# A seventh pair of heads ahead of the first feed-forward, and weight sizes on VectorE alone

## The chip, the core and the metric

One core of one Trainium2 chip runs the kernel. The metric is the device time of one execution in microseconds (us). Three timed runs of the kernel before are given, and one profiled execution of it.

## What is computed

`reference()` chains two parts. The first is attention in which a query sees only the keys of its own hash bucket; the second is a gated feed-forward with a convolution of three taps along the sequence.

```python
q_bits = (np.einsum('bhsd,dk->bhsk', q, proj) > 0)       # the same for k
mask = q_bucket[:, :, :, None] == k_bucket[:, :, None, :]
scores = np.where(mask, scale * np.matmul(q, k.transpose(0, 1, 3, 2)), -1000000000.0)
scores = scores - np.max(scores, axis=-1, keepdims=True)
attn = np.exp(scores); attn = attn / (np.sum(attn, axis=-1, keepdims=True) + 1e-09)
x = np.matmul(attn, v)                                    # heads side by side: [4, 768, 512]
h = np.maximum(x @ w_in, 0.0)                             # [512, 1024]
out = (h * sigmoid(conv3(h)) @ w_out)                     # [1024, 512]
```

There are 4 batches, 8 heads, 768 positions and 64 values per head. q, k and v are float32. The weights w_in, w_out and the taps come as 64-bit floats, which the kernel itself splits into two float32 parts.

## The kernel before

Heads go in pairs: 16 pairs, four per batch. A pair is 12 units, a unit being 128 queries of one head against 768 keys. For each unit TensorE makes the products (L286, into `s`), VectorE takes the row maximum while it copies them to `e` (L299), ScalarE takes the exponential with its sum (L306), and three units later TensorE transposes `e` (L329, into `t`), which ScalarE copies to `at` (L336). `s` and `t` share three PSUM buffers, so the next transposes wait until a maximum has emptied its buffer. Every fourth unit the matmuls with v follow for 256 queries (L355, into `v`): this unit is called a burst here.

The products use a bucket mask in extra rows. For that each pair's R (queries and keys, transposed) is loaded into one single buffer (L191); TensorE makes its hash (L219), VectorE and GpSimd turn it into `bits` (L222, L224), GpSimd splits R into a rounded high part `hi` (L204) and a low part that stays in R (L209), for one head and then for the other. DMAs of the SP queue, in program order, bring these to their rows (L207 `hi`, L211 R, L228 `bits`). `prepare` spreads these steps over units 1 to 7 of the pair in front; the other head's low part (the second L209) falls into the burst at unit 7, after which the next load of R is issued. The hash of a pair stands at unit 3 of the pair in front, in a burst.

The early pairs (six, up to the first feed-forward) leave the softmax's division to the end: VectorE makes reciprocals of the sums (L320, L321), GpSimd spreads them to 64 columns each (`rec`, L323), TensorE transposes them beside the values (L350, two per burst), ScalarE copies them out (L360), VectorE multiplies (`x`, L364), and GpSimd splits x into `xh` and `xl` (L365, L366). The later ten pairs are normalised on GpSimd before the transposes instead (L314).

The weights are 16 blocks of 128 x 512. For each one ScalarE takes the absolute value (L87), GpSimd clamps it (L90), VectorE makes the upper word (L95, L97) and the lower (L102, L104), ScalarE rounds the upper to the high part (L136), and GpSimd makes the low part (L139, L140). The upper word has two buffers. `background` issues these steps, 3.75 VectorE operations in each burst from unit 7 on, and what is left in the first feed-forward. Behind a burst's maximum VectorE's order is: x's product, then this lump of weight operations, then the next maximum.

The feed-forward of a batch follows two pairs (`DEFER`) behind the batch's last: after pairs 5, 9, 13 and 15, counted from 0. It has 16 steps of hidden matmuls (L393), convolution and gate, and output matmuls (L423). The first burst behind each feed-forward's start is the one of the last 256 queries. All engines run in the order in which the program is written.

## Time and profile before

| What | Value |
|---|---|
| three timed runs | 748.12, 752.3, 996.83 us; median 752.3 |
| the profiled execution | 750.76 us, its span 749.0 us |
| busy in the span | TensorE 714.4, VectorE 499.2, ScalarE 509.2, GpSimd 373.6 us |

An engine's busy time is the sum of its own instructions. A busy TensorE is not TensorE at its best, since matmuls are pipelined and a slow clock counts as busy. The order of time of an engine gives the start and the length of instructions of one kind in a row; in brackets stands how long the engine was idle before and who ended the wait. A row's name out<-in is that of the tiles.

### The profile page before, as it was taken

How to read it: one execution, taken by the hardware profiler on the slowest of the kernel's cores; microseconds unless marked ns; L12 is line 12 of the kernel's file. 1: busy time of each engine (PE TensorE's matmuls, PEld its weight loads, DVE VectorE, ACT ScalarE, POOL GpSimd, SP SyncE). 2: the span in 40 equal slices, each digit the busy share in tenths (PEclk: the TensorE clock that was granted, in tenths of full speed). 3: DMA queues.
4: the chain of work that ended last, by engine and by line, in shares of the span. 5: the costliest groups of instructions: out<-in, count | busy, mean ns of one | idle time of the engine just before them, and what ended most of it. 6: DMA issues, size and time to landing. Idle time of an engine off the chain costs nothing.

```text
span 749.0 us, 13385 instructions
## 1 busy us (share of the span) xinstructions
PE 714.4 (95%) x4588; PEld 587.5 (78%) x4588; DVE 499.2 (67%) x1195; ACT 509.2 (68%) x954; POOL 373.6 (50%) x372
## 2 busy tenths in 40 slices
PE   5989999988899999999999999999999999999997
PEld 3767777776679987777788988777788897778986
DVE  7588999977667656666657655665666665564663
ACT  5867887886655548778774557787785547785554
POOL 4366777756566324755735423656645323341221
PEclk8999999998999999999999999999999999999999
DMA  3876576553412102365441302255461211000011
GB/s 141 198 204 155 141 206 181 168 162 85 114 43 72 64 37 70 82 181 136 121 121 31 104 1 105 68 150 132 119 163 33 70 43 63 2 1 1 0 43 43
DMA packets 30357, 72.18 MB, mean 96 GB/s; under 512 B 5937, under 2 KB 7505, under 8 KB 30289
## 3 DMA queue, kind: packets, MB, share of 16 engines
q1 hardware_dynamic: 27696, 62.88, 30.9%
q10 hardware_dynamic: 2592, 8.44, 3.6%
q8 instruction: 37, 0.61, 0.3%
q14 instruction: 32, 0.25, 0.1%
HBM read 27.40 MB, written 6.29 MB: 45 GB/s over the span
## 4 chain that ended last, share of the span: by engine, by line
PE 69%; DVE 4%; POOL 4%; DMA 3%; ACT 1%; issue 1%; SPq 0%; POOLq 0%; DVEq 0%
PE o L423 18%; PE h L393 17%; PE s L286 11%; PE t L329 11%; PE v L355 11%; DVE e L299 2%; DMA k<-R 1%; DMA R<-in_qk 1%; PE hash L219 1%; POOL wuo L139 1%; POOL e L314 1%; POOL wo L140 1%; ACT e L306 1%; DVE wuo L97 1%; POOL R L209 1%
## 5 line engine op out<-in xcount | busy, mean ns | idle before, releaser
L299 DVE TENSOR_SCALAR_CACHE_REDUCE e<-s 128x768 f32<-128x768 f32 x192 | 183.3, 955 | 80.9 <-PE s L286 72.1
L306 ACT ACTIVATE e<-e,st 128x768 f32<-128x768 f32 x192 | 181.2, 944 | 23.1 <-DVE st L303 12.8
L336 ACT COPY at<-t 128x768 f32<-128x768 f32 x192 | 152.3, 794 | 47.3 <-PE t L329 47.1
L329 PE MATMUL t<-ident,e 128*128 128x128 f32 x1152 | 164.5, 280 | 19.9 <-DVE e L299 17.9
L314 POOL TENSOR_SCALAR e<-e,st 128x768 f32<-128x768 f32 x120 | 109.3, 911 | 117.3 <-ACT at L336 59.9
L329 PEld LDWEIGHTS t<-ident,e 128*128 128x128 f32 x1152 | 133.4, 144 | 42.6 <-DVE e L299 22.4
L402 DVE SCALAR_TENSOR_TENSOR ht<-ht,cw 128x384 f32<-128x384 f32 (+1 forms) x128 | 117.8, 921 | 70.0 <-ACT ht L400 66.8
L412 POOL TENSOR_TENSOR g<-ht,g 128x384 fp32r<-128x384 f32 x64 | 72.0, 1125 | 163.9 <-ACT g L411 129.7
L423 PE MATMUL o<-wo,g 128*128 128x512 f32 x576 | 143.3, 395 | 0.7 <-POOL g L412 0.7
L393 PE MATMUL h<-xh,wi 128*128 128x386 f32 x512 | 142.0, 340 | 0.0
L355 PE MATMUL v<-at,v 128*64 128x256 f32 x1152 | 134.9, 383 | 0.0
L423 PEld LDWEIGHTS o<-wo,g 128*128 128x128 f32 x576 | 107.0, 188 | 23.5 <-ACT ht L400 1.2
L286 PE MATMUL s<-K,Q 128*128 128x384 f32 x384 | 118.7, 391 | 1.0 <-POOL K L253 0.9
L355 PEld LDWEIGHTS v<-at,v 128*64 128x64 f32 x1152 | 78.7, 137 | 45.5 <-issue 10.9
L286 PE MATMUL s<-k,q 96*128 96x384 f32 x384 | 102.2, 348 | 2.2 <-DVE e L299 2.2
L405 ACT ACTIVATE ht<-ht 128x384 f32<-128x384 f32 x64 | 33.6, 525 | 96.4 <-DVE ht L402 96.4
L393 PEld LDWEIGHTS h<-xh,wi 128*128 128x128 f32 x512 | 94.0, 188 | 3.7 <-ACT ht L400 1.2
L393 PE MATMUL h<-xl,wi 128*128 128x386 f32 x256 | 86.8, 339 | 0.0
L286 PEld LDWEIGHTS s<-K,Q 128*128 128x128 f32 x384 | 60.1, 196 | 22.2 <-issue 17.4
L286 PEld LDWEIGHTS s<-k,q 96*128 96x128 f32 x384 | 72.9, 197 | 3.0 <-ACT q L266 3.0
L406 DVE TENSOR_TENSOR ht<-ht 128x384 f32<-128x384 f32 x64 | 41.5, 649 | 31.5 <-ACT ht L405 31.3
L209 POOL TENSOR_TENSOR R<-R,hi 128x768 fp32r<-128x768 f32 x30 | 60.4, 2014 | 0.9 <-PE hash L219 0.8
(75 smaller groups left out, 622.2 us busy)
## 6 DMA issues: line engine op xcount, KB each, us to landing
R<-in_qk SPq DMA_DIRECT2D x15, 768.0 KB
K<-hi SPq DMA_DIRECT2D x60, 192.0 KB
v<-in_v SPq DMA_DIRECT2D x16, 384.0 KB
out<-osb SPq DMA_DIRECT2D x24, 256.0 KB
Q<-hi SPq DMA_DIRECT2D x30, 192.0 KB
q<-hi SPq DMA_DIRECT2D x30, 192.0 KB
Q<-R SPq DMA_DIRECT2D x30, 192.0 KB
k<-R SPq DMA_DIRECT2D x30, 192.0 KB
```

Source lines behind the costliest of these rows:

```text
L209: nc.gpsimd.tensor_tensor(lo, R, hi.bitcast(F32), ALU.subtract)
L286: nc.tensor.matmul(self.sp[:, half, :HS], A[:, h, qs], C[:, h, half * HS:(half + 1) * HS], start=(kk == 0), stop=(kk == 1))
L299: nc.vector.tensor_scalar(self.e.rearrange("p (a b) -> p a b", a=2), self.sp[:, :, :HS], MASKED, None, ALU.max, ALU.max, accum_out=self.st ...
L306: nc.scalar.activation(self.e, self.e, AF.Exp, bias=self.st[:, 1:2], scale=SCALE, accum_out=self.sum)
L314: nc.gpsimd.tensor_scalar(self.e, self.e, self.st[:, 3:4], 0.0, ALU.mult, ALU.add)
L329: nc.tensor.transpose(self.tp[:, c // 3, c % 3 * P:(c % 3 + 1) * P], self.e[:, c * P:(c + 1) * P], ident)
L336: nc.scalar.copy(pr.at[self.h][:, :, :, self.tq * P:(self.tq + 1) * P], self.tp[:, :, :3 * P].rearrange("p j (c q) -> p j c q", c=3))
L355: nc.tensor.matmul(av[h * D:(h + 1) * D, :QB], vt[:, c, h, :], ats[h][:, c // 3, c % 3, :], start=(c == 0), stop=(c == NCK - 1), tile_posi ...
L393: nc.tensor.matmul(hp[:, :HW], w, x[:, c0:c0 + HW], start=(n == 0), stop=(n == 3 * NCC - 1))
L402: nc.vector.scalar_tensor_tensor(t[:, a:z], ht[:, o + k - 1 + a:o + k - 1 + z], cw[:, f, k:k + 1], t[:, a:z], ALU.mult, ALU.add)
L412: nc.gpsimd.tensor_tensor(g[:, 1, :], t, g[:, 0, :].bitcast(F32), ALU.subtract)
L423: nc.tensor.matmul(op, l, r, start=(f == 0 and n == 0), stop=(f == NFC - 1 and n == 2))
```

## The change

- `DEFER` goes from 2 to 3: the feed-forwards follow pairs 6, 10, 14 and 15, and seven pairs instead of six divide at the end.
- The size of a weight is made on VectorE: a bitwise and with 0x7FFFFFFF, and a maximum with the smallest size. The absolute value on ScalarE and the clamp on GpSimd go. A block has six VectorE operations, issued 5.2 to a burst, one less at a hash. GpSimd's two operations of a block are issued as soon as the block's last VectorE operation is. Upper and lower words, and the output copies, share four buffers (before: two and five).
- The sums have a second column that holds 1e-9, so one reduction adds it; the spreading on GpSimd goes. Four matmuls take a column of reciprocals, read 64 times, as the weight and the identity as the moving operand.
- x's product overwrites `rs` (two buffers); its two GpSimd operations are issued behind the burst's weight steps.
- `prepare` has two lists: the hash stays where all steps stood, ahead of the burst's value matmuls; the high and low parts of R go behind x's parts.
- The feed-forward's steps fetch no weights any more and issue one weight step instead of two.

```diff
--- before.py
+++ after.py
...
 LAG, EB = 3, 5
-DEFER = 2
+DEFER = 3
 FLAG = 3
 LATE = NP + DEFER
...
-RATE = 3.75
+RATE = 5.2
...
+    sums4 = [cp.tile([P, 2 * QB // P, 2], F32, name=f"sums{i}") for i in range(3)]
+    for t in sums4:
+        nc.gpsimd.memset(t, 1e-9)
...
-            self.up, self.low = (ring(wp, bufs, [P, WC], I32, f"w{x}", f"w{x}{name}")[:, :n]
-                                for x, bufs in (("u", 2), ("l", 5)))
+            self.low, self.up = (ring(wp, 4, [P, WC], I32, "w", f"{x}{name}")[:, :n] for x in ("low", "up"))
             self.upf, self.lowf = self.up.bitcast(F32), self.low.bitcast(F32)
 
-        def size(self):
-            nc.scalar.activation(self.lowf, self.hi.bitcast(F32), AF.Abs)
-
-        def clamp(self):
-            nc.gpsimd.tensor_scalar(self.lowf, self.lowf, F32_MAX, F64_MIN, ALU.min, ALU.max)
-
-        def upper(self):
+        def vector(self):
...
             V, up, low = nc.vector, self.up, self.low
+            V.tensor_scalar(low, self.hi, 0x7FFFFFFF, None, ALU.bitwise_and)
+            yield
+            V.tensor_scalar(self.lowf, self.lowf, F64_MIN, None, ALU.max)
+            yield
             V.tensor_scalar(low, low, 3, 0x3FFFFFFF, ALU.logical_shift_left, ALU.bitwise_and)
             yield
             V.scalar_tensor_tensor(up, self.hi, -0x40000000, low, ALU.bitwise_and, ALU.bitwise_or)
             yield
-
-        def lower(self):
-            V, up, low = nc.vector, self.up, self.low
             V.tensor_scalar(low, up, -0x800000, None, ALU.bitwise_and)
             yield
             V.scalar_tensor_tensor(self.lowf, self.lo, 2.0 ** -52, self.lowf, ALU.mult, ALU.mult)
...
     def split_weights():
-        todo, ends = [], None
-        def ahead():
-            if fetched:
-                raw, name = fetched.pop(0)
-                todo.append(Decode(raw, WC, name))
-                todo[-1].size()
-        ahead()
-        ahead()
-        yield
-        for d in todo:
-            d.clamp()
-        yield
-        while todo:
-            d = todo.pop(0)
-            ahead()
-            yield from d.upper()
-            if ends:
-                ends()
-            if len(todo) == 2:
-                todo[-1].clamp()
-            yield from d.lower()
-            blk = weights[d.name] = cp.tile([P, 2, WC], F32R, tag=f"w{d.name}", name=f"w{d.name}")
+        while fetched:
+            raw, name = fetched.pop(0)
+            d = Decode(raw, WC, name)
+            yield from d.vector()
+            blk = weights[name] = cp.tile([P, 2, WC], F32R, tag=f"w{name}", name=f"w{name}")
             nc.scalar.copy(blk[:, 0, :], d.upf)
-            def ends(d=d, blk=blk):
-                nc.gpsimd.tensor_tensor(d.upf, d.upf, blk[:, 0, :].bitcast(F32), ALU.subtract)
-                nc.gpsimd.tensor_tensor(blk[:, 1, :], d.upf, d.lowf, ALU.add)
-        ends()
+            nc.gpsimd.tensor_tensor(d.upf, d.upf, blk[:, 0, :].bitcast(F32), ALU.subtract)
+            nc.gpsimd.tensor_tensor(blk[:, 1, :], d.upf, d.lowf, ALU.add)
+            yield
...
-            for now in ((sa,), (), (hs, sa), (hs,), (sb,), (), (sb,)):
-                for g in now:
-                    next(g, None)
-                yield
+            def steps(plan):
+                for g in plan:
+                    if g:
+                        next(g, None)
+                    yield
+            return steps((None, None, hs, hs)), steps((sa, None, sa, None, sb, None, sb))
...
         def reciprocals(self):
 
             pr = self.pair
-            sums = self.sums
-            nc.vector.tensor_scalar(sums, sums, 1e-9, None, ALU.add)
-            nc.vector.reciprocal(sums, sums)
-            pr.rec = ring(wp, 1, [P, QB // P, 2, D], F32, "rec", f"rec{self.nm}")
-            nc.gpsimd.tensor_scalar(pr.rec, sums.unsqueeze(3).to_broadcast([P, QB // P, 2, D]), 1.0, 0.0,
-                                    ALU.mult, ALU.add)
+            pr.inv = ring(wp, 2, [P, 2 * QB // P], F32, "inv", f"inv{self.nm}")
+            nc.vector.tensor_reduce(pr.inv, self.sums, mybir.AxisListType.X, ALU.add)
+            nc.vector.reciprocal(pr.inv, pr.inv)
...
             for t in range(QB // P):
-                nc.tensor.transpose(av[:, QB + t * P:QB + (t + 1) * P],
-                                    rec[:, t].rearrange("p h d -> p (h d)"), ident)
+                for h in range(2):
+                    nc.tensor.matmul(av[h * D:(h + 1) * D, QB + t * P:QB + (t + 1) * P],
+                                     inv[:, 2 * t + h:2 * t + h + 1].to_broadcast([P, D]), ident,
+                                     start=True, stop=True, tile_position=(0, h * D))
...
         def out():
-            x = ring(wp, 1, [P, QB], F32, "x32", f"x{pr.nm}_{qb}")
-            nc.vector.tensor_tensor(x, av[:, :QB], rs, ALU.mult)
-            nc.gpsimd.tensor_scalar(xh[:, cols], x, 1.0, 0.0, ALU.mult, ALU.add)
-            nc.gpsimd.tensor_tensor(xl[:, cols], x, xh[:, cols].bitcast(F32), ALU.subtract)
+            nc.vector.tensor_tensor(rs, av[:, :QB], rs, ALU.mult)
+        def parts():
+            nc.gpsimd.tensor_scalar(xh[:, cols], rs, 1.0, 0.0, ALU.mult, ALU.add)
+            nc.gpsimd.tensor_tensor(xl[:, cols], rs, xh[:, cols].bitcast(F32), ALU.subtract)
...
-        rs = ring(wp, 1, [P, QB], F32, "rs", f"rs{pr.nm}_{qb}")
-        return [spread, *chunks], (factors, out)
+        rs = ring(wp, 2, [P, QB], F32, "rs", f"rs{pr.nm}_{qb}")
+        return [spread, *chunks], (factors, out, parts)
...
-            fetch(1)
             background(1)
             if i >= 3:
-                next(prep[0], None)
+                prepare(0)
+                prepare(1)
...
             if i < len(todo):
                 gs.append(next(run[i]))
-            background(1)
...
+        parts = []
         if burst:
-            for high, low in lows:
+            for high, low, part in lows:
                 low()
+                parts.append(part)
             lows = []
         if u and k == PREP and pi + 1 < len(pairs):
-            prep[0] = pairs[pi + 1].prepare()
-        next(prep[0], None)
+            prep[:] = pairs[pi + 1].prepare()
+        prepare(0)
+        if ending:
+            prepare(0)
         for _ in range(1 + NCK if ending else AVS[(i - LAG) % 4]):
             if av:
                 steps, last = av[0]
...
                     outs.append(last)
                     av.pop(0)
         if burst and i >= W0:
-            background(RATE)
+            background(RATE - (k == PREP + 2))
+        for last in parts:
+            last()
+        prepare(1)
```

VectorE in the burst at unit 7 of the sixth pair (1_1): `x` and `rs` are the product of the values, `wl`, `wu` or `low`, `up` a block's lower and upper words, `e` the next units. Before:

```order
L364 TENSOR_TENSOR x1_0_2_2208<-v1_0_2_2047,rs1_0_2_2048 128x256
L102 TENSOR_SCALAR wlo5_1857<-wuo5_1856 128x512
L104 SCALAR_TENSOR_TENSOR wlo5_1857<-rawo5_1601,wlo5_1857 128x512
L95 TENSOR_SCALAR wlo6_1977<-wlo6_1977 128x512
L97 SCALAR_TENSOR_TENSOR wuo6_1976<-rawo6_1731,wlo6_1977 128x512
L299 TENSOR_SCALAR e1_1_4_0_2252,st1_1_4_0_2250<-s1_1_4_0_2245 128x768
L303 TENSOR_SCALAR st1_1_4_0_2250<-st1_1_4_0_2250 128x1
```

and now:

```order
L333 TENSOR_TENSOR rs1_0_2_2019<-v1_0_2_2018,rs1_0_2_2019 128x256
L93 TENSOR_SCALAR lowo4_2072<-lowo4_2072 128x512
L95 TENSOR_SCALAR lowo4_2072<-lowo4_2072 128x512
L97 SCALAR_TENSOR_TENSOR upo4_2073<-rawo4_1471,lowo4_2072 128x512
L99 TENSOR_SCALAR lowo4_2072<-upo4_2073 128x512
L101 SCALAR_TENSOR_TENSOR lowo4_2072<-rawo4_1471,lowo4_2072 128x512
L270 TENSOR_SCALAR e1_1_4_0_2221,st1_1_4_0_2220<-s1_1_4_0_2215 128x768
```

Four weight operations of three blocks became five of one block, whose size is made here too. Whatever stands between x's product and the next `e` delays that maximum.

GpSimd in the same burst: `hi` and R are the parts for the next pair, `w...` the weight block, `xh` and `xl` the parts of x. Before:

```order
L204 TENSOR_SCALAR hi1_2_1_2160<-R1_2_1863 128x768
L365 TENSOR_SCALAR xh1_0_1808<-x1_0_2_2208 128x256
L366 TENSOR_TENSOR xl1_0_1809<-x1_0_2_2208,xh1_0_1808 128x256
L209 TENSOR_TENSOR R1_2_1863<-R1_2_1863,hi1_2_1_2160 128x768
L139 TENSOR_TENSOR wuo4_1722<-wuo4_1722,wo4_2102 128x512
L140 TENSOR_TENSOR wo4_2102<-wuo4_1722,wlo4_1723 128x512
L90 TENSOR_SCALAR wlo7_2105<-wlo7_2105 128x512
```

and now:

```order
L171 TENSOR_SCALAR hi1_2_1_2129<-R1_2_1838 128x768
L111 TENSOR_TENSOR upo4_2073<-upo4_2073,wo4_2199 128x512
L112 TENSOR_TENSOR wo4_2199<-upo4_2073,lowo4_2072 128x512
L336 TENSOR_SCALAR xh1_0_1779<-rs1_0_2_2019 128x256
L337 TENSOR_TENSOR xl1_0_1780<-rs1_0_2_2019,xh1_0_1779 128x256
L176 TENSOR_TENSOR R1_2_1838<-R1_2_1838,hi1_2_1_2129 128x768
```

R's low part stood ahead of the two weight operations and stands behind them and behind x's parts now; the clamp of a later block (L90) is gone. L111 reads what ScalarE rounds after the block's last VectorE operation.

## Rows read from the trace of the kernel before

**Rows 1.** The page's part 1: busy us, share of the span, instructions of each engine.
```profile
PE 714.4 (95%) x4588; PEld 587.5 (78%) x4588; DVE 499.2 (67%) x1195; ACT 509.2 (68%) x954; POOL 373.6 (50%) x372
```

**Rows 2.** TensorE in order of time: start us, us, line, operation, tiles, count.
```profile
24.76 2.81 PE L355 MATMUL v<-at,v 128*64 128x256 f32 x24
...
207.44 2.81 PE L355 MATMUL v<-at,v 128*64 128x256 f32 x24
...
634.26 2.81 PE L355 MATMUL v<-at,v 128*64 128x256 f32 x24
...
642.78 2.81 PE L355 MATMUL v<-at,v 128*64 128x256 f32 x24
```

**Rows 3.** Who TensorE waited for: us in total, times, longest us.
```profile
PE t L329 <- DVE e L299: 17.9, 13, 3.5
...
PE hash L219 <- DMA R<-in_qk: 2.1, 4, 1.0
```

**Rows 4.** VectorE in order of time, 185 to 192 us; idle time in brackets.
```profile
185.50 0.94 DVE L95 TENSOR_SCALAR wlo<-wlo 128x512 int32<-128x512 int32 x1
190.73 0.69 DVE L97 SCALAR_TENSOR_TENSOR wuo<-rawo,wlo 128x512 int32<-128x512 int32 x1 [4.29 <-POOL wo L140]
191.34 0.95 DVE L299 TENSOR_SCALAR_CACHE_REDUCE e<-s 128x768 f32<-128x768 f32 x1
```

**Rows 5.** GpSimd in order of time, the same stretch.
```profile
186.12 2.00 POOL L209 TENSOR_TENSOR R<-R,hi 128x768 fp32r<-128x768 f32 x1
188.08 1.28 POOL L139 TENSOR_TENSOR wuo<-wuo,wo 128x512 f32<-128x512 f32 x1
189.44 1.26 POOL L140 TENSOR_TENSOR wo<-wuo,wlo 128x512 fp32r<-128x512 f32 x1
```

**Rows 6.** Busy us and TensorE's granted clock (PEclk) by stretch.
```profile
186.00:188.50 2.50, 2.50 (x20) 2.07 (x16) 0.44 (x1) 0.96 (x3) 2.50 (x3) 1.00 0.93 219
...
192.40:196.20 3.80, 3.80 (x18) 3.70 (x19) 2.86 (x10) 3.02 (x6) 0.49 (x2) 0.59 0.68 216
```

**Rows 7.** TensorE in order of time, the hashes of four pairs.
```profile
46.96 0.85 PE L219 MATMUL hash<-R,hw_sb 128*32 128x384 f32 x8 [1.02 <-DMA R<-in_qk]
...
79.02 0.85 PE L219 MATMUL hash<-R,hw_sb 128*32 128x384 f32 x8
...
108.98 0.85 PE L219 MATMUL hash<-R,hw_sb 128*32 128x384 f32 x8
...
169.68 0.85 PE L219 MATMUL hash<-R,hw_sb 128*32 128x384 f32 x8
```

**Rows 8.** GpSimd in order of time, the pair between two hashes.
```profile
92.96 2.01 POOL L209 TENSOR_TENSOR R<-R,hi 128x768 fp32r<-128x768 f32 x1
...
108.45 0.83 POOL L204 TENSOR_SCALAR hi<-R 128x768 fp32r<-128x768 f32 x1 [0.61 <-DMA R<-in_qk]
```

**Rows 9.** The SP queue in order of time, the same pair.
```profile
88.29 0.78 SPq L228 DMA_DIRECT2D k<-bits  x1
...
97.22 0.74 SPq L211 DMA_DIRECT2D Q<-R  x1
```

**Rows 10.** VectorE in order of time, a swollen operation and an undisturbed lump.
```profile
82.20 1.95 DVE L102 TENSOR_SCALAR wli<-wui 128x512 int32<-128x512 int32 x1
...
100.53 0.42 DVE L364 TENSOR_TENSOR x<-v,rs 128x256 f32<-128x256 f32 x1
100.87 0.42 DVE L95 TENSOR_SCALAR wli<-wli 128x512 int32<-128x512 int32 x1
...
103.97 0.96 DVE L299 TENSOR_SCALAR_CACHE_REDUCE e<-s 128x768 f32<-128x768 f32 x1
```

**Rows 11.** TensorE behind that lump.
```profile
105.13 0.82 PE L329 MATMUL t<-ident,e 128*128 128x128 f32 x6
```

**Rows 12.** ScalarE in order of time, the rounded copy of a block.
```profile
185.61 0.62 ACT L136 CAST wo<-wuo 128x512 fp32r<-128x512 f32 x1 [0.26 <-DVE wlo L104]
```

**Rows 13.** Groups by line: us in all, mean ns, idle before.
```profile
L350 PE MATMUL v<-ident,rec 128*128 128x128 f32 x36 | 7.2, 280 | 0.0
```

More of the change, by code (lines that the diff above doesn't have):

```diff
@@ L104, in lower, with split_weights @@
             V.scalar_tensor_tensor(self.lowf, self.lo, 2.0 ** -52, self.lowf, ALU.mult, ALU.mult)
[L105 to L142 removed]
+    def split_weights():
+        while fetched:
[3 more added lines that the diff above has]
+            blk = weights[name] = cp.tile([P, 2, WC], F32R, tag=f"w{name}", name=f"w{name}")
+            nc.scalar.copy(blk[:, 0, :], d.upf)
+            nc.gpsimd.tensor_tensor(d.upf, d.upf, blk[:, 0, :].bitcast(F32), ALU.subtract)
+            nc.gpsimd.tensor_tensor(blk[:, 1, :], d.upf, d.lowf, ALU.add)
+            yield
     def decode_taps(raw):
         d = Decode(raw, NFC * 3, "cw")
[L146 removed]
+        yield from d.vector()
         yield
[L148 to L151 removed]
         nc.vector.tensor_tensor(cw.rearrange("p f k -> p (f k)"), d.upf, d.lowf, ALU.add)
@@ L180, in __init__ @@
             self.late = b * NP + p >= LATE
-            self.rec = None
+            self.inv = None
         def load(self):
@@ L259, in prepare_now @@
                     yield
-                bits = ring(wp, 5, [P, WC], I32, "wl", f"bits{nm}_{h}").bitcast(F32)[:, :HS]
+                bits = ring(wp, 4, [P, WC], I32, "w", f"bits{nm}_{h}").bitcast(F32)[:, :HS]
                 nc.vector.tensor_scalar(bits, hps[h], 0.0, cst[:, 2:3], ALU.is_gt, ALU.subtract)
@@ L293, in maximum @@
             if self.tq == 0 and self.h == 0 and not pr.late:
-                pr.sums = ring(wp, 3, [P, QB // P, 2], F32, "sums", f"sums{self.nm}")
+                pr.sums = sums4[self.qb % 3]
             self.sums = None if pr.late else pr.sums
-            self.sum = self.st[:, 2:3] if pr.late else pr.sums[:, self.tq, self.h:self.h + 1]
+            self.sum = self.st[:, 2:3] if pr.late else pr.sums[:, 2 * self.tq + self.h, 0:1]
             e = wp.tile([P, 776], F32, tag="e", name=f"e{self.nm}", bufs=EB)
@@ L337, in to_sbuf, with values @@
                            self.tp[:, :, :3 * P].rearrange("p j (c q) -> p j c q", c=3))
-    def values(pr, qb, ats, rec):
+    def values(pr, qb, ats, inv):
         if qb == 0:
@@ L376, in values, with prepare @@
         if pr.late:
-            return chunks, (out_high, out_low)
-        rs = ring(wp, 1, [P, QB], F32, "rs", f"rs{pr.nm}_{qb}")
-        return [spread, *chunks], (factors, out)
-    g2, prep = [None], [iter(())]
+            return chunks, (out_high, out_low, lambda: None)
+        rs = ring(wp, 2, [P, QB], F32, "rs", f"rs{pr.nm}_{qb}")
+        return [spread, *chunks], (factors, out, parts)
+    g2, prep = [None], [iter(()), iter(())]
+    def prepare(part):
+        next(prep[part], None)
     def hidden(b, half, f, xs):
@@ L426, in output @@
             for m in range(HS // P):
-                osb = ring(wp, 5, [P, WC], I32, "wl", f"osb{b}_{half}_{m}").bitcast(F32)
+                osb = ring(wp, 4, [P, WC], I32, "w", f"osb{b}_{half}_{m}").bitcast(F32)
                 copy = nc.vector.tensor_copy if m == 2 else nc.scalar.copy
@@ L484, in lsh_attention_conv_ffn @@
         burst = AVS[(i - LAG) % 4] > 0
-        for high, low in outs:
+        for high, low, part in outs:
             high()
@@ L492, in lsh_attention_conv_ffn @@
         if ending:
-            for high, low in lows:
+            for high, low, part in lows:
                 low()
+                part()
             lows = []
@@ L511, in lsh_attention_conv_ffn @@
             next(first, None)
+        parts = []
         if burst:
-            for high, low in lows:
+            for high, low, part in lows:
                 low()
+                parts.append(part)
             lows = []
         if u and k == PREP and pi + 1 < len(pairs):
-            prep[0] = pairs[pi + 1].prepare()
-        next(prep[0], None)
+            prep[:] = pairs[pi + 1].prepare()
+        prepare(0)
+        if ending:
+            prepare(0)
         for _ in range(1 + NCK if ending else AVS[(i - LAG) % 4]):
@@ L538, in lsh_attention_conv_ffn @@
             if not ending:
-                av.append(values(w.pair, w.qb, w.pair.at, w.pair.rec))
+                av.append(values(w.pair, w.qb, w.pair.at, w.pair.inv))
             else:
                 def fill():
-                    steps, last = values(w.pair, w.qb, w.pair.at, w.pair.rec)
+                    steps, last = values(w.pair, w.qb, w.pair.at, w.pair.inv)
                     for step in [*steps, *last]:
```

12 lines of the change are left out of this document (2 added, 10 removed).

## Prediction

> **What bounds the kernel now.** I read the page first: TensorE is busy for 95% of the span [rows 1], so a large gain can only be work that TensorE no longer waits for or no longer does slowly. The second view is TensorE's own order of time, and in it the start of every group of value matmuls (a burst, one in four units). From 24.76 to 207.44 us, that is up to the burst inside the first feed-forward, there are 18 of them, so 17 periods in 182.7 us, 10.75 us each. Late in the kernel the same four units take 8.52 us (634.26 to 642.78) [rows 2]. So the stretch ahead of the first feed-forward, in which the weights are decoded, loses about 2 us in each burst; behind it attention is TensorE's own work, and nothing that the change does can shorten that.
>
> The third view, who waited for whom on TensorE, gives the loss its name: the transposes waited for VectorE's row maximum 13 times, 17.9 us in total and 3.5 us at the longest [rows 3]. One such wait followed through: behind the maximum of one unit VectorE has the lump of weight operations. It finished L95 at about 186.4, as the start and the length say, then stood idle for 4.29 us in front of L97, and the next maximum started at 191.34 [rows 4]. It waited for GpSimd's L140, because L97 writes one of two upper-word buffers and L140 is the last reader of that buffer. GpSimd was at work all that time, in its order: 2.00 us for the low part of R, then 1.28 and 1.26 us for a weight block [rows 5]. And after the wait TensorE ran slowly: the granted clock was 1.00 before it and 0.59 in the 3.8 us behind it [rows 6], most of them at the lower of its two levels (1.2 of 2.4 GHz). 3.8 us at 0.59 are some 1.5 us lost, so a long stall is paid about one and a half times.
>
> **There is a second loop that the page does not show.** R has one buffer. From a pair's hash the way leads over the hash bits on GpSimd (their first DMA is issued at 88.29), the SP queue, the low part of R (GpSimd, 92.96), its DMAs (issued at 97.22), the next load of R to its landing, for which GpSimd's next high part waited until 108.45, and the next hash at 108.98 [rows 7 to 9]. From the hash at 79.02 to 108.45 is 29.4 us. TensorE waited little for it, 2.1 us in four waits [rows 3], but only because the pairs themselves took (169.68 - 46.96)/4 = 30.7 us [rows 7]. Whoever makes the early pairs faster than 29.4 us meets this loop.
>
> **The change, part by part.**
>
> *One more pair ahead of the first feed-forward.* Three bursts are added ahead of it and three are taken away behind the third feed-forward, where a burst costs 8.52 us [rows 2]: 25.6 us off at the end. One hash leaves the third feed-forward too and comes to the early pairs: 0.8 us more off [rows 7]. Together -26.4. The seventh pair also takes the deferred normalisation instead of GpSimd's; GpSimd has room there, so that is counted at nothing, and if it had none, the early stretch would show it.
>
> *The weights' sizes on VectorE.* Sixteen ScalarE and sixteen GpSimd operations go and 32 of VectorE's come. Those that go lay beside the value matmuls, off VectorE, which is what the transposes waited for [rows 3]; they are counted at nothing. A block now has four tensor_scalar operations and two with two inputs, in 96 steps; 20 bursts at 5.2, less one at a hash, give 97, so the decoding is over when the first feed-forward starts. An undisturbed tensor_scalar is 0.42 us [rows 10]. For the first one, which reads every second word, no row exists: from 0.42 to the 0.7 us of the two-input form L97 [rows 4]; I take 0.42, the same kind of operation. Five operations with x's product are then some 3.1 us. At 100.53 a lump of 3.44 us (to the maximum at 103.97) left no wait in front of the transposes at 105.13 [rows 11], while the lumps that did cost were swollen: L102 took 1.95 us at 82.20 [rows 10]. So the new lump fits into the cover of the value matmuls if it isn't swollen; each microsecond over about 3.5 is TensorE's.
>
> The Trainium skill, SBUF — State Buffer, section "Who interferes with whom", says that a VectorE operation in a two-port mode, or with two SBUF inputs, locks out GpSimd, and that whichever comes second blocks until the first is done. By that rule the change is partly against itself, since it moves work from ScalarE, which shares no port, to operations of just this kind; the 1.95 beside the 0.42 us agrees. Taken at its worst, every one of the 32 added operations blocked by 1.5 us, it gives VectorE 48 us more, of which the cover takes a part; by the undisturbed row it is 32 x 0.42 = 13 us, all under the cover. It is part of the slow rival below.
>
> *Order on GpSimd.* The two weight operations now stand right behind the block's end, x's parts behind them, and R's low part last; before, R's low part came ahead of the weights. So the wait on the two upper buffers goes: a block's buffers are used again two blocks, more than one burst, later. What is late next is R. Its low part now waits for the block's last VectorE operation (the first to the fifth of the lump, 0.7 to 3.1 us), for ScalarE's rounded copy (0.62 [rows 12]), and for 1.28 + 1.26 us of weights [rows 5]: 3.8 to 6.2 us later than before in its burst. Before, it was done at 92.96 + 2.0, 2.3 us ahead of the SP queue that sends it at 97.22 [rows 8, 9]; and the stall of some 1.5 us ahead of it in that pair goes. So the sending moves by 3.8 - 2.3 - 1.5 = 0 to 6.2 - 2.3 - 1.5 = 2.4 us, and the loop is 29.4 to 31.8 us. In two of the six early pairs no block ends beside the hash, which brings the bits forward by some 3 us (the copy and two weight operations), but R's low part of the other head still follows a block's end; and the loads of weights, which share the DMA engines, are over by half of the pairs. I take 30.4, one above the measured loop.
>
> *Broadcast weight.* Two 128-row transposes become four 64-row matmuls, in pairs on two halves of the columns. Before, 36 records took 7.2 us [rows 13], 0.4 a burst. After, between half of that (two at once, each as long as one before) and twice it (one after the other); I take 0.43 us a burst, as before, by the same row. Inside the wait for R it costs nothing; without that cover the upper end is 20 x 0.4 = 8 us, which the range keeps. The broadcast on GpSimd goes with it, off the path.
>
> *The sum.* The chain up to the hash at 46.96 is SP's and stays [rows 7]. Five loops of 30.4 put the seventh hash at 199.0. From there to the burst in the feed-forward: before, 207.44 - 169.68 = 37.8 us, with the two longest stalls in it. Now three bursts of 8.52, 1.2 for the hash and the start, 1.3 for the spreading, 1.5 us for what is left of VectorE's stalls: 29.6. The burst comes at 228.6, that is 21.1 later than 207.44. 21.1 - 26.4 = -5.3. Against the profiled execution (750.76 us, 1.8 of it outside the span) that is 745.5; its time lies between the lower two of the runs shown (748.1 and 752.3, the latter the median), so 745 stands against the median as 1.0% less.
>
> **Rivals.**
>
> *R does not bind; VectorE's stalls just go.* Then a pair costs three bursts of 8.52, the hash 0.8, the spreading 1.3 and some 0.7 of leftover: 28.3. 46.96 + 5 x 28.3 + 29.6 = 218.1, +10.7 against before, and the time is 750.8 + 10.7 - 26.4 = 735. For it: TensorE waited for R only 2.1 us in all [rows 3], and the loop has slack on SP. Against it: the one loop that the rows close is 29.4 us [rows 7 to 9], more than 28.3, and the change delays a link of it.
>
> *The loop grows and the clock falls: slower than before.* The place is the hash, where TensorE arrives after 28 us and waits 2 to 3 us for R; behind such a gap it ran at the lower level [rows 6], which delays the burst that R's low part hangs on, while the added two-port operations block on GpSimd (1.5 us each, as in [rows 10]) and delay the block's end. Price: 1.5 for the clock and 1.5 for one blocked operation in each of five pairs on top of 30.4: 33.4, so 15 us more, 760. It decides from 31.5 us a pair on, where +26.4 eats the pair that was taken away at the end. For it: both pieces are seen in the trace. Against it: GpSimd now stands waiting while most of a lump runs, so there is less to block on.
>
> *The decoding isn't finished in time.* 97 steps for 96 leave no room, but the last blocks are w_out's, first used several microseconds into the feed-forward; nothing is lost unless several blocks are missing. No time of its own.
>
> **How the numbers follow.** The forecast (R's loop, 740 to 751) has a chance of 0.52, the fast rival 0.32, the slow one 0.16. The range 730 to 757 takes in the fast rival's 735 with a few us for its leftover, and the slow one's lower half. A change of 2%, 15 us, is about what a measurement of this kernel can tell from none: faster by more than that is below 737, most of the fast rival and little else, 0.28; slower by more is above 767, the end of the slow rival, 0.03; the rest 0.69.
>
> **What would show it.** Right: gaps of 1 to 3 us in front of the hash, put down to the DMA of R; hashes 30 to 31 us apart; GpSimd's low part of R behind the weights; VectorE with no wait for GpSimd in its lumps; the burst in the first feed-forward near 229 us; stretches behind it unchanged but for one pair less. Wrong: hashes 28 us apart without a gap (fast rival), or lumps over 4.5 us and the low clock level after each hash (slow rival); wrong altogether if the feed-forwards or the late pairs change.

## The result, and the profile after

The kernel after took 742.46 us in the median of its runs (739.48 to 799.68), the kernel before 750.33 in runs beside it: a ratio of 0.9895, 95% interval 0.9866 to 0.9925. One run of each kernel, 799.68 and 996.83 us, was slow and is left out of the ratio. The profiled execution took 739.48 us, its span 737.5. Because its early stretch turned out fast, the same kernel was profiled a second time among the experiments (span 742.3); both are read here.

TensorE in the page's part 1, and who it waited for, in the kernel after:

```profile
PE 710.9 (96%) x4720; PEld 589.0 (80%) x4720; DVE 487.3 (66%) x1211; ACT 498.5 (68%) x937; POOL 331.9 (45%) x334
...
PE hash L186 <- DMA R<-in_qk: 9.1, 9, 2.2
...
PE t L297 <- DVE e L270: 1.1, 3, 0.6
```

The two rows changed places. The transposes' waits for VectorE's maximum went from 17.9 us to 1.1, and the hash's waits for R from 2.1 to 9.1 [rows 3]. VectorE no longer stands in front of a weight operation for GpSimd, as in [rows 4]; no such line is left among its waits.

TensorE in order of time (start, length, line), the rows that answer to [rows 2, 7]:

```profile
25.26 2.76 PE L325 MATMUL v<-at,v 128*64 128x256 f32 x24
...
43.35 0.85 PE L186 MATMUL hash<-R,hw_sb 128*32 128x384 f32 x8
...
192.02 0.85 PE L186 MATMUL hash<-R,hw_sb 128*32 128x384 f32 x8 [1.87 <-DMA R<-in_qk]
...
220.17 0.85 PE L186 MATMUL hash<-R,hw_sb 128*32 128x384 f32 x8 [1.48 <-DMA R<-in_qk]
...
223.74 2.76 PE L325 MATMUL v<-at,v 128*64 128x256 f32 x24
...
299.53 2.84 PE L325 MATMUL v<-at,v 128*64 128x256 f32 x24
```

From the second hash (43.35, called the first early hash below) to the seventh there are five pairs of 29.7 us. The burst in the first feed-forward comes at 223.74, 16.3 us later than before, and a pair less stands behind the third one.

GpSimd and the SP queue in one of these pairs:

```profile
147.05 1.27 POOL L111 TENSOR_TENSOR upo<-upo,wo 128x512 f32<-128x512 f32 x1 [5.96 <-ACT wo L110]
148.40 1.28 POOL L112 TENSOR_TENSOR wo<-upo,lowo 128x512 fp32r<-128x512 f32 x1
...
150.83 1.84 POOL L176 TENSOR_TENSOR R<-R,hi 128x768 fp32r<-128x768 f32 x1
...
161.98 0.83 POOL L171 TENSOR_SCALAR hi<-R 128x768 fp32r<-128x768 f32 x1 [1.91 <-DMA R<-in_qk]
```

```profile
152.70 0.46 SPq L178 DMA_DIRECT2D Q<-R  x1
...
156.39 0.38 SPq L158 DMA_DIRECT2D R<-in_qk  x1
```

GpSimd now waits for ScalarE's copy with R's low part behind it in its order; SP sends the low part (152.70) the moment it is done (152.67), and the load of R follows when the copies have landed, which the next high part and the next hash wait for.

### The profile page after: what moved, and what is told of

Its sections match the earlier page's. It is cut to its first block, busy times and chain, and to the rows that moved or that the text cites. A ratio compares the mean times of both kernels' runs of the same rounds, so it can differ in the third digit from the quotient of the medians.

```text
span 737.5 us, 13543 instructions
## 1 busy us (share of the span) xinstructions
PE 710.9 (96%) x4720; PEld 589.0 (80%) x4720; DVE 487.3 (66%) x1211; ACT 498.5 (68%) x937; POOL 331.9 (45%) x334
## 4 chain that ended last, share of the span: by engine, by line
PE 69%; DMA 11%; POOL 7%; issue 5%; DVE 4%; SPq 3%; ACT 1%; POOLq 0%; DVEq 0%; ACTq 0%
PE h L368 19%; PE o L398 18%; PE v L325 11%; PE s L257 10%; PE t L297 9%; DMA R<-in_qk 6%; DMA k<-R 4%; POOL R L176 2%; SPq L174 2%; DVE e L270 1%; DMA K<-hi 1%; PE hash L186 1%; POOL hi L171 1%; ACT e L277 1%; SPq L178 1%
## 5 line engine op out<-in xcount | busy, mean ns | idle before, releaser
L297 PE MATMUL t<-ident,e 128*128 128x128 f32 x1152 | 160.0, 275 | 3.6 <-POOL e L285 1.5
L377 DVE SCALAR_TENSOR_TENSOR ht<-ht,cw 128x384 f32<-128x384 f32 (+1 forms) x128 | 114.7, 896 | 71.2 <-ACT ht L375 69.0
L297 PEld LDWEIGHTS t<-ident,e 128*128 128x128 f32 x1152 | 130.6, 141 | 22.3 <-POOL e L285 7.4
L285 POOL TENSOR_SCALAR e<-e,st 128x768 f32<-128x768 f32 x108 | 98.3, 911 | 103.1 <-DVE st L284 51.4
L257 PE MATMUL s<-K,Q 128*128 128x384 f32 x384 | 116.7, 385 | 1.9 <-ACT e L277 1.0
L325 PEld LDWEIGHTS v<-at,v 128*64 128x64 f32 x1152 | 81.2, 138 | 42.4 <-issue 8.6
L257 PE MATMUL s<-k,q 96*128 96x384 f32 x384 | 100.2, 342 | 2.1 <-ACT q L237 1.9
L257 PEld LDWEIGHTS s<-k,q 96*128 96x128 f32 x384 | 70.7, 191 | 3.5 <-ACT q L237 3.0
L176 POOL TENSOR_TENSOR R<-R,hi 128x768 fp32r<-128x768 f32 x30 | 56.6, 1886 | 0.2
```

The source lines that it names most:

```text
L176: nc.gpsimd.tensor_tensor(lo, R, hi.bitcast(F32), ALU.subtract)
L257: nc.tensor.matmul(self.sp[:, half, :HS], A[:, h, qs], C[:, h, half * HS:(half + 1) * HS], start=(kk == 0), stop=(kk == 1))
L285: nc.gpsimd.tensor_scalar(self.e, self.e, self.st[:, 3:4], 0.0, ALU.mult, ALU.add)
L297: nc.tensor.transpose(self.tp[:, c // 3, c % 3 * P:(c % 3 + 1) * P], self.e[:, c * P:(c + 1) * P], ident)
L325: nc.tensor.matmul(av[h * D:(h + 1) * D, :QB], vt[:, c, h, :], ats[h][:, c // 3, c % 3, :], start=(c == 0), stop=(c == NCK - 1), tile_posi ...
L377: nc.vector.scalar_tensor_tensor(t[:, a:z], ht[:, o + k - 1 + a:o + k - 1 + z], cw[:, f, k:k + 1], t[:, a:z], ALU.mult, ALU.add)
```

## The experiments

Ratios are to the kernel before, run on the same chip beside them. "R loop" is the chain of the single buffer of R.

**1. R by halves, one buffer each.** The first head's half is loaded as soon as that half is free, on the same SP queue.

```diff
-            self.R = ring(wp, 1, [P, 2, S], F32R, "R", f"R{nm}")
+            self.R.append(ring(wp, 1, [P, S], F32R, f"R{h}", f"R{h}{self.nm}"))
...
+        if u and k == PREP + 4 and pi + 2 < len(pairs):
+            pairs[pi + 2].load_r(0)
```

> The changed kernel with R as two buffers, one per head, of half the size each (no more memory): the first head's half of the next R is loaded after unit 5 of the pair in front, only the second head's half after unit 7. Theory (the loop of R binds the early pairs): the load that ends the loop is half as long, so TensorE's waits for R in front of the hash fall from 9.1 us in 9 to under 4, the seven early hashes come 28 to 28.7 us apart instead of 29.5, and the time is 4 to 9 us below the changed kernel's 742 (ratio to before 0.978 to 0.985). Rival (the waits for R only fill slack that another limit, VectorE's or GpSimd's work of a burst, would take): the waits move elsewhere and the ratio stays at 0.9895 within 0.003.

Measured: 747.12 us, 0.9958 (0.9926 to 0.999); a miss in the time, by the theory and by the rival, though the waits for R fell as expected, to 2.3 us. In the early pairs hash to hash is 29.1 us ((191.61 - 46.02)/5), yet the burst in the first feed-forward stands at 224.16, between the two profiles of the kernel after (223.74 and, run 9, 227.41): ahead of it TensorE now waited 5.8 us for ScalarE and 1.7 for the copy `Q<-R`. The late pairs became slower: from the first burst behind the first feed-forward to the one in the second it took 102.6 us, where the two profiles after have 98.8 and 100.3. SP around a late pair, first after, then with halves:

```profile
333.88 0.55 SPq L178 DMA_DIRECT2D Q<-R  x1
334.48 0.61 SPq L178 DMA_DIRECT2D k<-R  x1
...
338.96 0.38 SPq L158 DMA_DIRECT2D R<-in_qk  x1
```

```profile
334.37 0.71 SPq L160 DMA_DIRECT2D R<-in_qk  x1
335.18 0.81 SPq L177 DMA_DIRECT2D Q<-R  x1
336.04 0.59 SPq L177 DMA_DIRECT2D k<-R  x1
...
342.51 0.33 SPq L160 DMA_DIRECT2D R<-in_qk  x1
```

The first half's load goes out right ahead of the second low part's copies; from the last of these to the load that waits for them it is 6.5 us instead of 4.5. Less was left to load, and it started 3.6 us later. So the late loop was not made shorter, and in the early pairs other waits took the place of the one for R. What the loop is worth this run doesn't show.

**2. R's parts ahead of the weights again** on GpSimd (`prepare(1)` moved before `background`).

> The changed kernel with R's high and low parts issued ahead of the burst's weight operations again, as before the change; all else as changed. Theory (R's low part behind the weights and x's parts on GpSimd lengthens the loop of R by up to 2 us): the low part is sent some 2 us earlier, the waits for R at the hash shrink by half, but GpSimd's 2 us now lie beside VectorE's lump and block it, so TensorE's waits for VectorE come back (1.1 us in the changed kernel, 5 to 12 here); in sum within 0.5% of the changed kernel, ratio to before 0.985 to 0.995. Rival (the order on GpSimd doesn't matter): both waits stay as they are, 9.1 and 1.1 us.

Measured: 740.32 us, 0.9863 (0.9835 to 0.9892). Waits of TensorE:

```profile
PE hash L186 <- DMA R<-in_qk: 8.4, 7, 2.7
...
PE t L297 <- DVE e L270: 3.2, 5, 0.9
```

The time is where it was expected, the waits are not: half of the 9.1 us was expected, and 5 to 12 us for VectorE. The pair is 29.4 us ((192.30 - 45.07)/5), against 29.7 and 30.1 in the two profiles after. By this the order that the change chose costs 0.3 to 0.6 us a pair in the R loop and saves 2 us of VectorE's waits; two profiles of one kernel differ by as much, and in the time these runs resolve no difference.

**3. Six pairs again** (`DEFER = 2`, `RATE = 6.1`), the rest of the change kept.

> The changed kernel with the first feed-forward after the sixth pair again (DEFER 2), the weight operations at 6.1 a burst so that they are done in 17 bursts. Theory (an early pair is bound by R's loop, 29.5 us, a late one by TensorE, 26.4): the seventh pair by itself costs 3 us, it only gives the weight operations room; with six to a burst the lumps are 0.6 us longer, part of which hides in the waits for R: 738 to 745, ratio 0.983 to 0.993. Rival (the gain came from the seventh pair, because more bursts share the decoding): this is slower than the changed kernel by 5 us or more, ratio over 0.996.

Measured: 746.11 us, 0.994 (0.9912 to 0.9968), between the two expectations; waits for the maximum are back at 6.6 us in 11 waits. Against before that leaves 0.6% for the other edits together, and against after (0.9895 and, below, 0.9908) some 0.3 to 0.45% for the seventh pair. The intervals overlap, so this split is no more than a reading.

**4. The spreading on GpSimd again** with two transposes (`rec`), instead of the broadcast weight.

> The changed kernel with the reciprocals spread by GpSimd and transposed by TensorE again in place of the broadcast weight. Theory (both forms lie inside other waits): the same as the changed kernel within 0.3%, ratio 0.987 to 0.993. Rival (GpSimd's 0.4 us a burst and its wait for the reciprocals delay R's low part or the bits): 2 to 4 us more, ratio 0.993 to 0.996, with the hashes 0.4 us further apart.

Measured: 743.07 us, 0.9903 (0.9871 to 0.9935), the same as after. TensorE then waited 7.4 us for `rec` and no less for R (9.0), while its matmuls of the spreading took 9.1 us instead of 13.8. Hash to hash is 30.1 us, as in run 9: the pairs became neither shorter nor longer by it.

**5. Two buffers for the first half of R**, so that its load waits for nothing; the room came from one buffer of `rs` and from starting constants.

```diff
+            self.R.append(ring(wp, 2 - h, [P, S], F32R, f"R{h}", f"R{h}{self.nm}"))
...
-        rs = ring(wp, 2, [P, QB], F32, "rs", f"rs{pr.nm}_{qb}")
+        rs = ring(wp, 1, [P, QB], F32, "rs", f"rs{pr.nm}_{qb}")
```

> The kernel after, with the raw pair R split by head: two buffers for the first head's half (loaded three units into the pair before, with nothing to wait for) and one for the second's; the room comes from one buffer of rs and from starting constants that lie in the last weight block's place. Theory (the loop hash, high part, low part, copies landed, load of 768 KB landed is what TensorE waits for in the stretch of the decode): only 384 KB stand at the loop's end, so TensorE's waits for R fall from 9.1 us to under 4, hash to hash falls from 29.7 us to 28.0 to 28.8, the fill burst comes at 216 to 220 us instead of 223.7, ratio to before 0.980 to 0.986. Rival (TensorE is bound there by its own work and the hash's wait only takes the place of another): hash to hash stays at 29.2 or more, the wait reappears at the next pair's first product, ratio 0.987 to 0.993.

Measured: 786.49 us, 1.0474 (1.0424 to 1.0523). The wait for R was gone (0.4 us), and a worse one had come: ScalarE's copy L332 (of the factors to `rs`) waited for GpSimd, and TensorE behind it.

```profile
ACT rs L332 <- POOL xl L339: 61.3, 16, 4.2
...
PE s L259 <- ACT at L306: 34.5, 15, 3.2
```

**6. One buffer of `rs`, nothing else**, to see whether that alone did it.

> The kernel after with one buffer of rs instead of two, nothing else; settles why the run with halves of R and one rs was slow (1.047, ScalarE waited 61 us for the low part of x on GpSimd). Theory (ScalarE's copy of the factors into the one rs waits for GpSimd's last read of it, which stands behind two weight operations of 1.27 us each; the transposes' copies queue behind it): ScalarE waits 45 to 65 us for GpSimd there, TensorE waits over 20 us for the transposes' copy, ratio 1.03 to 1.055. Rival (the halves of R did it): ratio 0.985 to 0.997.

Measured: 783.03 us, 1.0413 (1.0389 to 1.0437). The theory held: ScalarE waited 57.0 us for GpSimd's read of `rs`, which the change has put behind two weight operations. Of the loss of run 5 nearly all is this buffer; the second buffer of `rs` in the diff belongs to the new order on GpSimd.

**7. Two whole buffers of R, with six pairs**, which leave room for it (run 3 plus one word of the code).

```diff
-            self.R = ring(wp, 1, [P, 2, S], F32R, "R", f"R{nm}")
+            self.R = ring(wp, 2, [P, 2, S], F32R, "R", f"R{nm}")
```

> First feed-forward after the sixth pair again (the weights' operations 6.1 a burst), and the room that this gives is used for a second whole buffer of R; to be held against the run with the sixth pair alone (0.994, TensorE waited 7.6 us for R and 6.6 us for the maximum on VectorE). Theory (R is the bound): the wait for R falls under 1.5 us, the waits for the maximum stay at 5 to 9 us, ratio 0.983 to 0.989. Rival (with six pairs VectorE's operations bind as soon as R doesn't): waits for the maximum grow past 12 us, ratio 0.991 or more.

Measured: 734.79 us, 0.98 (0.9741 to 0.9859); faster than before, and than the kernel after beside it (0.9908, run 9). The hashes and the burst in the first feed-forward in run 3, then here:

```profile
45.26 0.85 PE L186 MATMUL hash<-R,hw_sb 128*32 128x384 f32 x8 [1.68 <-ACT at L304]
...
195.79 1.51 PE L186 MATMUL hash<-R,hw_sb 128*32 128x384 f32 x8 [3.39 <-DMA R<-in_qk]
...
201.78 2.76 PE L325 MATMUL v<-at,v 128*64 128x256 f32 x24
```

```profile
PE t L297 <- DVE e L270: 6.6, 10, 2.1
...
PE hash L186 <- DMA R<-in_qk: 2.5, 2, 1.6
...
42.73 0.85 PE L186 MATMUL hash<-R,hw_sb 128*32 128x384 f32 x8
...
191.07 0.85 PE L186 MATMUL hash<-R,hw_sb 128*32 128x384 f32 x8 [1.65 <-DMA R<-in_qk]
...
194.66 2.76 PE L325 MATMUL v<-at,v 128*64 128x256 f32 x24
```

Only R's buffer differs from run 3. The wait for R fell from 7.6 to 2.5 us while VectorE's stayed at 6.6, and the time fell by 1.4%, more than expected: the burst in the first feed-forward stands at 194.66 instead of 201.78, 7.1 of the 10.1 us between the spans (742.5 and 732.4); the other 3.0 came behind it. Of the 7.1 us, 2.5 stand ahead of the first early hash (in run 3 GpSimd's next high part waited for R's DMA up to 45.20, so that hash waited for R too), 2.2 lie in the five pairs, and 2.4 between the seventh hash and the burst: behind the wait of 3.39 us the granted clock of run 3 was 0.50 from 196 to 200 us, behind the 1.65 us here it was 1.00. So with six pairs the R loop is shown, and it costs more than the waits put down to it.

Two things it doesn't show. Without the loop the pairs are still 29.7 us ((191.07 - 42.73)/5), so the next bound stands close behind; VectorE's 6.6 us are the largest wait left. And for seven pairs no run shows the gain: runs 1, 5 and 10 took most of the wait for R away (2.3, 0.4 and 1.9 us were left), and in each other waits came.

**8. The sizes on ScalarE and GpSimd again**, one block ahead, seven pairs kept.

```diff
-            V.tensor_scalar(low, self.hi, 0x7FFFFFFF, None, ALU.bitwise_and)
-            V.tensor_scalar(self.lowf, self.lowf, F64_MIN, None, ALU.max)
+            nc.scalar.activation(self.lowf, self.hi.bitcast(F32), AF.Abs)
+            nc.gpsimd.tensor_scalar(self.lowf, self.lowf, F32_MAX, F64_MIN, ALU.min, ALU.max)
```

> The kernel after with the weights' sizes made on ScalarE and the clamp on GpSimd again, one block ahead (four operations of a block left on VectorE, 4.4 steps a burst); seven pairs and the broadcast weight stay. Theory (the gain has two parts of about the same size, the seventh pair and the sizes on VectorE; six pairs alone gave 0.994): waits of VectorE for a clamp or an upper word on GpSimd come back, at least 3 us of them passed on to TensorE as waits for the maximum, ratio 0.992 to 0.997. Rival (the slower pace alone took the waits away, where a size is made doesn't matter): TensorE waits under 2 us for the maximum, ratio 0.987 to 0.991.

Measured: 770.43 us, 1.0259 (1.0211 to 1.0306), worse than theory and rival. VectorE, then TensorE:

```profile
DVE lowo L97 <- POOL lowo L90: 24.9, 6, 4.2
...
PE t L307 <- DVE e L280: 24.1, 8, 4.0
```

GpSimd at one such wait (VectorE's L97 came at 110.38):

```profile
107.00 1.28 POOL L119 TENSOR_TENSOR upi<-upi,wi 128x512 f32<-128x512 f32 x1 [2.98 <-ACT wi L118]
108.36 1.28 POOL L120 TENSOR_TENSOR wi<-upi,lowi 128x512 fp32r<-128x512 f32 x1
109.73 0.61 POOL L90 TENSOR_SCALAR lowo<-lowo 128x512 f32<-128x512 f32 x1
```

Where a lump goes on with the next block, that block's clamp stands behind the two weight operations of the one just ended, and VectorE waits 4.16 us. Before, clamps ran two blocks ahead with seven word buffers; whether seven pairs leave room for that was not tried. So the run shows what making the sizes elsewhere costs with one block of lead, not the worth of the edit as such.

**9. The kernel after once more.**

> The kernel after itself, unchanged, beside the three others, for its profile a second time: ratio 0.986 to 0.993; TensorE waits 8 to 10 us for R; if the early first hash (43.4 us, forecast 47.0) belongs to the kernel it stands between 43 and 44 us again, if it is chance it lies between 44 and 47.

Measured: 744.46 us, 0.9908 (0.9873 to 0.9943). Its rows, with the load of R for the first early hash and GpSimd's next high part, which waits for it:

```profile
38.95 0.39 SPq L158 DMA_DIRECT2D R<-in_qk  x1
...
45.16 0.83 POOL L171 TENSOR_SCALAR hi<-R 128x768 fp32r<-128x768 f32 x1 [3.25 <-DMA R<-in_qk]
45.22 0.85 PE L186 MATMUL hash<-R,hw_sb 128*32 128x384 f32 x8 [1.64 <-ACT at L304]
...
195.62 0.85 PE L186 MATMUL hash<-R,hw_sb 128*32 128x384 f32 x8 [1.87 <-DMA R<-in_qk]
...
227.41 2.76 PE L325 MATMUL v<-at,v 128*64 128x256 f32 x24
```

The same load in the first profile after, then in the kernel before:

```profile
38.52 0.39 SPq L158 DMA_DIRECT2D R<-in_qk  x1
...
42.89 0.83 POOL L171 TENSOR_SCALAR hi<-R 128x768 fp32r<-128x768 f32 x1 [1.22 <-DMA R<-in_qk]
```

```profile
40.74 0.39 SPq L191 DMA_DIRECT2D R<-in_qk  x1
```

The kernel's early pairs are not the same in each execution: here 30.1 us each and a first early hash 1.9 us later. That is R's load: from issue to landing it took 4.4 us there, 6.2 here (and 6.2 before, 40.74 to 46.90). So of the 43.35 those 1.9 us are chance; that the load is issued about 2 us earlier than before is the same in both profiles. The profile puts three of the early waits at the hash, 5.1 us, down to ScalarE here, but GpSimd's next high part waits for R's DMA up to the same moment, as in these rows; TensorE's 7.5 us for R (8 to 10 were expected) leave them out. TensorE's clock was 0.82 in this profile's first 17 us and 1.00 in the other's; that alone doesn't set the hash, for run 3 had 1.00 there too, with the hash at 45.26.

**10. Halves of R as in run 5, with two `rs`**; the hash's bits take a turn in the ring of four word buffers instead.

> The kernel after with seven pairs, both buffers of rs and two buffers for the first head's half of R again (one for the second's); the room comes from the hash's sign bits, which take a turn in the ring of four word buffers of the weights instead of a buffer of their own. Theory (the loop of R is what binds): TensorE's waits for R fall from 7.5 to 9 us to under 3, hash to hash from 29.7 or 30.1 us to under 29, ratio to before 0.978 to 0.986. Rival (the bits hold a word buffer for some 15 us and VectorE's decode stands behind it, or halves shift the wait to the next product): waits for the maximum over 6 us or hash to hash at 29.5 or more, ratio 0.988 to 1.0.

Measured: 753.55 us, 1.0034 (1.0006 to 1.0063): the rival, a little beyond its range, with 30.8 us from hash to hash. VectorE's weight operations waited 4.0 us for the bits' DMA and 3.0 us for GpSimd. A wait of 2 us is paid more than once when the clock falls behind it (the columns as in [rows 6]):

```profile
194.00:196.00 2.00, 0.59 (x6) 0.35 (x4) 1.36 (x5) 2.00 (x5) 0.10 (x1) 1.00 1.06 238
...
198.00:200.00 2.00, 2.00 (x9) 1.91 (x9) 1.12 (x3) 0.05 (x1) 0.00 (x0) 0.50 0.60 177
```

**11. Run 7 with R's parts first on GpSimd.**

> Six pairs and two whole buffers of R (0.980), with R's parts ahead of the weights' operations on GpSimd as before the change. Theory (with two buffers the order of R on GpSimd no longer matters for the loop, and putting it first only delays the weights): waits for R as they were, 2 to 3 us, waits for the maximum 6 to 10 us, ratio 0.979 to 0.987. Rival (copies of the next pair still come late for its first products, and R first helps them): ratio 0.970 to 0.977.

Measured: 740.15 us, 0.9843 (0.9816 to 0.987). Waits for the maximum went up to 13.0 us, beyond what was expected, those for R down to 0.7. Without the R loop the order that the change chose looks the better one (734.79 us in run 7); the intervals of the two ratios overlap.

**12. Run 7 with each load of R three units earlier**, since its buffer is free.

> Six pairs and two whole buffers of R as in the run at 0.980, with each load of R issued three units earlier in the pair (its buffer has been free since the pair before). Theory (the 2.5 us that TensorE still waited for R there are loads issued late, behind the copies of the second low part on SP): no wait for R over 0.5 us, waits for the maximum on VectorE unchanged at 6 to 9 us, ratio 0.974 to 0.981. Rival (the early 768 KB shares the DMA engines with the copies that the next products need): a wait of the first products or of VectorE takes its place, ratio 0.982 to 0.99.

Measured: 762.28 us, 1.0144 (1.0108 to 1.018): the rival, and more than it gave. No wait for R was left, but:

```profile
183.56 0.52 SPq L158 DMA_DIRECT2D R<-in_qk  x1
...
187.10 0.70 SPq L178 DMA_DIRECT2D Q<-R  x1
...
194.82 0.98 PE L257 MATMUL s<-K,Q 128*128 128x384 f32 x2 [3.52 <-DMA Q<-R]
```

The 768 KB go out on the same queue ahead of the copies that the next pair's first product needs; in five pairs that product waited for `Q<-R`, 9.4 us in all. That the low-part copies sit behind the load's transfers is the reading of these rows; the Trainium skill (DMA: Bandwidth & Descriptors, section "Queues, rings and completion order") says that each DMA engine takes the descriptors of a queue in the order of its ring, which agrees. The late load in run 7 is not an oversight.

## Why the prediction was right

The forecast was 745 us for a kernel bound by R's loop; the medians are 742.46 and 744.46. The mechanism is what both profiles after show, and the terms can be held against them:

| Term, us | forecast | after | after again |
|---|---|---|---|
| first early hash | 46.96 | 43.35 | 45.22 |
| five loops | 152.0 | 148.7 | 150.4 |
| seventh hash to the burst in the first feed-forward | 29.6 | 31.7 | 31.8 |
| that burst at | 228.6 | 223.7 | 227.4 |
| from it to the next burst (77.9 before) | 77.9 | 75.8 | 75.8 |
| from there to the end (463.6 - 26.4) | 437.2 | 438.0 | 439.1 |
| span | 743.7 | 737.5 | 742.3 |

- *VectorE's stalls go.* Right: 1.1 us for 17.9 [rows 3], no wait for GpSimd in a lump, and hardly a lump over the cover. The runs separate the edits that did it only in part: with six pairs 6.6 us are left (run 3).
- *R's loop, 30.4 us (29.4 to 31.8).* Right: 29.7 and 30.1, with gaps in front of the hash in which R's DMA was awaited, and the low part behind the weights. In the first profile these gaps are 6.6 us in the five pairs; without them a pair is 28.4 us, the fast rival's work. That the loop costs time run 7 shows for six pairs; for seven it rests on the profiles. The link that the change delays was sized a little high: 0.3 to 0.6 us by run 2, where 1.0 was taken.
- *"The chain up to the hash at 46.96 is SP's and stays."* Wrong by 1.7 to 3.6 us. The load that this hash waits for goes out some 2 us earlier than before in both profiles (the cause is open), and its landing adds a chance of another 2 us (run 9). One row was taken as fixed.
- *The tail of 29.6.* Wrong by 2.1 us. It counted one hash, but an eighth stands ahead of the last burst, at 220.17, and waits 1.48 us for R as well: 0.85 + 1.48 is about the miss. The second `prepare(0)` under `if ending:` in the diff puts it there; before, it stood inside the first feed-forward:

```profile
216.73 0.85 PE L219 MATMUL hash<-R,hw_sb 128*32 128x384 f32 x8
```

- *The stretches behind unchanged but for one pair less.* Not quite. The first feed-forward became 2.1 us shorter: 0.85 is that hash, 0.70 a wait for GpSimd at 223.16 that is gone, and the rest is open (run 3 has 75.8 too, so it is not the seventh pair). So 0.85 of the miss in the tail and of this one is the same hash, once too many and once too few. The stretch from there to the end became 0.8 to 1.9 us longer than forecast; from 300 us on TensorE waited 2.1 and 3.1 us at hashes, where it had been 0.8 before.
- *Sizes at nothing.* Not settled. The `and` that had no row took 0.42 us undisturbed, the value chosen. But one operation that went did not lie off VectorE: before, VectorE waited 4.62 us for a clamp, and the transposes behind it 1.75 us:

```profile
29.75 0.82 DVE L95 TENSOR_SCALAR wli<-wli 128x512 int32<-128x512 int32 x1 [4.62 <-POOL wli L90]
```

- *Broadcast weight at nothing.* Right. The four matmuls take 13.8 us in 21 bursts, 0.66 each where 0.43 was taken, and run 4 finds no difference in the time.
- *The slow rival* (a gap, then the low clock, and blocked operations). Its pieces are real, and one place in the first profile has both: behind the wait of 2.18 us ahead of the hash at 73.51 the granted clock was 0.73 and then 0.50 from 74 to 78 us, the value matmuls took 4.45 us instead of 2.76, and L95 took 1.92 us. The second profile has the low clock behind the hashes at 75.66 and 136.36. But it did not come in each pair, the waits at the hash stayed at 2.6 us and less, and the granted clock over the early stretch was 0.99 (0.98 in the second profile), where it had been 0.95 before:

```profile
25.30:223.70 198.40, 187.89 (x1502) 150.25 (x1498) 159.27 (x408) 149.97 (x281) 105.84 (x108) 0.99 0.61 165
```

The Trainium skill's rule that a VectorE operation in a two-port mode and one of GpSimd lock each other out (SBUF — State Buffer, section "Who interferes with whom") agrees with the rows of the new operation: it took 0.42 us at 155.40, where GpSimd stood idle, and 0.94 at 181.58, beside the last 0.66 us of GpSimd's low part of R.

```profile
155.40 0.42 DVE L91 TENSOR_SCALAR lowo<-rawo 128x512 int32<-128x512 int32 x1
...
181.58 0.94 DVE L91 TENSOR_SCALAR lowo<-rawo 128x512 int32<-128x512 int32 x1
```

Fewer operations were met that way than before. The 96 weight operations of VectorE took 59.5 us, 10.5 more than at the undisturbed 0.42 and 0.69 us; the 64 of before took 65.3 us, 29.8 more. So VectorE's part became shorter although 32 operations came, which fits what the prediction held against this rival, that GpSimd stands waiting while most of a lump runs.

- *The fast rival* (R doesn't bind) is not this kernel. Run 7 has its time, 735 us, but not its pairs: they are 29.7 us, not 28.3. The change took away VectorE's stalls and ran into R's loop, as forecast; the sum of -5.3 us came out as -6.7 in the second profile and -11.5 in the first, which had the early start.

That the sum comes so near is in part luck: in the second profile the terms miss by -1.7, -1.6, +2.2, -2.1 and +1.9 us, about -1.4 in all.

## What to carry to other kernels

Before an edit that speeds up a stretch, walk once round every buffer that exists only once: its loop, not the engine that waits most, can be the next bound, and the page shows hardly a trace of it while something else is slower. A buffer taken away to make room for an experiment has a loop too (one `rs` made the kernel after 5% slower), and a load issued earlier than needed competes with the copies needed sooner. A wait that an edit takes away is not yet time: here others stood close behind. Where a forecast hangs on a single row of a start-up stretch, its chance spread belongs into the range.

## What was not expected of the hardware

The same kernel's early stretch differed by 3.7 us between two profiles (223.74 and 227.41), which is half of the gain to be measured. And two gaps of nearly one length went differently: behind a wait of 1.82 us at 133.70 in the kernel after the clock stayed at 1.00, behind one of 2.14 us in run 7 it fell to 0.53 and 0.62, near the lower of the two levels, for about 4 us. Behind 1.96 us at 136.36 in the second profile of the kernel after it fell to 0.50 too. The rows, behind the 1.82 us and then in run 7:

```profile
134.00:136.00 2.00, 2.00 (x26) 1.21 (x20) 1.36 (x2) 0.00 (x0) 1.92 (x4) 1.00 0.76 248
```

```profile
130.00:132.00 2.00, 2.00 (x11) 1.96 (x10) 1.30 (x4) 1.97 (x4) 0.83 (x1) 0.53 0.01 3
132.00:134.00 2.00, 2.00 (x13) 1.72 (x16) 1.10 (x4) 1.38 (x4) 0.00 (x0) 0.62 0.54 117
```
